# Attention and gated MLP in one kernel: in the assembling of the 64-bit weights the maximum with a constant is taken by GpSimd, beside a minimum with a very large number

## Chip, core and metric

The kernel runs on one core of one Trainium2 chip. The metric is the device time of one execution in microseconds (us). Engines are named as in the profile: PE is TensorE (matmuls), PEld its weight loads, DVE is VectorE, ACT is ScalarE, POOL is GpSimd, SP is SyncE, which here issues the DMAs.

## What is computed

The reference is a block-causal attention over 8 batches and 8 heads of 576 positions of 64 dimensions, and then a gated MLP without a nonlinearity of its own.

```python
scores = scale * np.matmul(q, k.transpose(0, 1, 3, 2))
scores = np.where(block_i >= block_j, scores, -1000000000.0)   # blocks of 64
attn = np.exp(scores - np.max(scores, axis=-1, keepdims=True))
attn = attn / (np.sum(attn, axis=-1, keepdims=True) + 1e-09)
x = np.matmul(attn, v)        # transposed and reshaped to (4608, 512)
a = x @ w1                    # 512 x 1024
b = x @ w2                    # 512 x 1024
h = a * b @ w3                # 1024 x 1024
out = (h @ w_out).astype(np.float32)   # 1024 x 512
```

The four weight matrices come in 64-bit floating point. The kernel reads them as pairs of 32-bit words and makes 32-bit values of them on the chip.

## The kernel before

The work is cut into 32 pairs of heads (`pair(n)`, four pairs to a batch). The first four pairs run beside the loading of the weights: this is the **loading stage**, some 165 us long. The generator `gen_w` goes through 40 pieces of weights of 128 x 512 values (8 of w_out, 16 of w3, 8 of w1, 8 of w2). Each piece goes through `load_w`:

- L133, a DMA issued by SP, brings 512 KB into a tile `wraw`, of which there are five;
- L138, ACT takes the absolute value of the high words into a tile `wbits`, of which there are six;
- L139, the maximum of that with 2^-15, in place;
- L140, DVE shifts the bits left by 3 and masks them;
- L141, DVE brings in the top bits of the high word;
- L144, DVE brings in the top bits of the low word; the result goes into `wo` (w_out), `w` (the w3 tile, printed as w3 in lists of instructions) or stays in `wbits`.

L139 and L140 read and write one 128 x 512 tile in SBUF; L141 and L144 read two tiles in SBUF. For w1 and w2 (`load_split`) ACT then rounds the piece (L150) and POOL subtracts the rounded from the full value (L151). For w3, PE multiplies it with w_out (L364), ACT and DVE split the product into a high and a low part (L352, L353). Beside this the first four pairs go through their attention: row maxima on DVE (L186), score and value matmuls on PE (L235, L275), exponentials on ACT (L243), splitting of q and k on ACT and POOL (L160, L209, L212), transposes on DVE (L315, L328), normalization (L329: POOL in pairs 0 and 1, DVE in pairs 2 and 3), and splitting of x (L338 on ACT, L339 on POOL).

In the loading stage the order on every engine is set by the scheduler of the language, which models the program; each engine then runs its own list in order, and an instruction that waits holds up all behind it on its engine. After the loading stage comes the **steady stage**: pairs 4 to 31 with the MLP filled in between their steps, with the order of PE written out by hand (`PLAN`).

Of the kernel before, what the change touches and what calls it, by code (L numbers as in the profile page):

```python
# [12 lines left out]
ALU = mybir.AluOpType  # L13
# [45 lines left out]
def block_causal_attention__then__gated_mlp_kernel(ctx, tc, qkv, consts, ident_in, w1, w2, w3t, wout, out_t):  # L59
    nc = tc.nc  # L60
# [64 lines left out]
    def load_w(dst, src, k):  # L125

        t = tl["early"].tile([P, 1024], F32, tag="wraw", name="wraw", bufs=5)  # L130
        u = tl["early"].tile([P, 512], F32, tag="wbits", name="wbits", bufs=6)
        wide = t.bitcast(I32)
        nc.sync.dma_start(out=wide.rearrange("p (k w) -> p k w", k=k), in_=src)  # L133
        wide = wide.rearrange("p (c two) -> p c two", two=2)
        low, high = wide[:, :, 0], wide[:, :, 1]
        bits = u.bitcast(I32)
        V = nc.vector
        nc.scalar.activation(u, high.bitcast(F32), AF.Abs)  # L138
        V.tensor_scalar(out=u, in0=u, scalar1=2.0**-15, scalar2=None, op0=ALU.max)  # L139
        V.tensor_scalar(out=bits, in0=bits, scalar1=3, scalar2=0x3FFFFFF8, op0=ALU.logical_shift_left, op1=ALU.bitwise_and)  # L140
        V.scalar_tensor_tensor(out=bits, in0=high, scalar=-0x40000000, in1=bits, op0=ALU.bitwise_and, op1=ALU.bitwise_or)  # L141
        if dst is None:
            dst = u.unsqueeze(1)
        V.scalar_tensor_tensor(out=dst.bitcast(I32), in0=low.rearrange("p (k w) -> p k w", k=k), scalar=29,  # L144
                               in1=bits.rearrange("p (k w) -> p k w", k=k), op0=ALU.logical_shift_right, op1=ALU.bitwise_or)
        return u

    def load_split(dst_h, dst_l, src):
        val = load_w(None, src.unsqueeze(1), 1)
        nc.scalar.copy(dst_h, val)  # L150
        nc.gpsimd.tensor_tensor(out=dst_l, in0=val, in1=dst_h, op=ALU.subtract)  # L151
# [190 lines left out]
    def gen_w(wp):  # L342
        wo = tl["wo"]
        for k in range(NF):
            load_w(wo[:, k : k + 1, :], wout[k * P : (k + 1) * P, :].unsqueeze(1), 1)
            yield
# [8 lines left out]
        for m in range(NF):  # L355
            t3 = wp.tile([P, NF, P], F32, tag="w3", name="w3", bufs=2)
            for k in range(0, NF, 4):
                src = w3t[k * P : (k + 4) * P, 2 * m * P : 2 * (m + 1) * P].rearrange("(k p) f -> p k f", p=P)
                load_w(t3[:, k : k + 4, :], src, 4)
                if k == 0:  # L360
                    yield
            acc = ps_m.tile([P, 512], F32, tag="psm", name=f"w{m}")
            for k in range(NF):
                nc.tensor.matmul(acc, t3[:, k, :], wo[:, k, :], start=(k == 0), stop=(k == NF - 1))  # L364
            pending.append((m, acc))
            if len(pending) > 1:
                evacuate()
            yield
            next(rows1)
            yield  # L370
# [172 lines left out]
```

## Time and profile before

| | us |
|---|---|
| median of 3 runs | 1035.99 |
| lowest and highest run | 1034.48, 1037.31 |
| the profiled execution's own time | 1035.29 |
| its span, first to last instruction | 1033.5 |

Busy time over the span: PE 977.6 us (95%), DVE 777.6 us (75%), POOL 605.2 us (59%), ACT 594.3 us (58%). A share over the whole span is an average of two stages: in the steady stage PE is busy nearly throughout, in the loading stage it is not. The table is read with the views by stretch, below.

### The profile page before, as it was taken

Reading aid. Unit: us, or ns where it says so; the run is one execution under the profiler, and the core shown is the slowest. Engines: PE = TensorE matmul, PEld = TensorE weight load, DVE = VectorE, ACT = ScalarE, POOL = GpSimd, SP = SyncE. Lnnn points to the kernel's source line nnn. Section 1 sums busy time; section 2 is a strip of 40 time slices with the busy share of each in tenths; the row PEclk is TensorE's granted clock in tenths of the full one; section 3 lists DMA queues with packets and bytes.
Section 4 is the critical chain, followed back from the end, with each engine's and each line's share of the span. In section 5 each row is a group of like instructions: output and inputs, shape, how many; then the busy total and the mean of one; then the engine's idle time right before and its main releaser. Section 6 shows DMA issues by size and latency. Waiting matters only on the chain.

```text
span 1033.5 us, 18295 instructions
## 1 busy us (share of the span) xinstructions
PE 977.6 (95%) x6624; PEld 891.3 (86%) x6624; DVE 777.6 (75%) x1376; ACT 594.3 (58%) x1505; POOL 605.2 (59%) x631
## 2 busy tenths in 40 slices
PE   2789788999999999999999999999999999999998
PEld 1444347999999999999999999999999999999998
DVE  7999997878788777778777788877777877785100
ACT  4746467666665666566565656665565566654221
POOL 3334367757676766767575767666676757673211
PEclk9889899999999999999999999999999999999999
DMA  6655421111110111111111110111111111000000
GB/s 209 220 184 182 156 94 37 37 59 37 60 36 19 43 42 55 42 54 38 60 37 60 37 50 17 42 49 43 54 38 59 36 61 36 25 1 24 1 24 23
DMA packets 27195, 61.52 MB, mean 60 GB/s; under 512 B 3360, under 2 KB 19872, under 8 KB 27104
## 3 DMA queue, kind: packets, MB, share of 16 engines
q1 hardware_dynamic: 27104, 60.35, 17.5%
q8 instruction: 52, 0.85, 0.3%
q14 instruction: 39, 0.32, 0.1%
HBM read 50.76 MB, written 9.44 MB: 58 GB/s over the span
## 4 chain that ended last, share of the span: by engine, by line
PE 53%; DVE 25%; ACT 12%; issue 7%; DMA 2%; POOL 1%; DVEq 0%; ACTq 0%; SPq 0%; POOLq 0%
PE ab L387 20%; PE o L403 17%; DVE pl L253 6%; PE s L235 6%; PE x L291 5%; DVE g L394 3%; ACT ph L251 3%; PE mx L182 3%; ACT xlow L322 2%; ACT p L250 2%; DVE wbits L141 2%; DVE m L186 2%; DVE wbits L139 2%; DVE hi L160 2%; PE w L364 1%
## 5 line engine op out<-in xcount | busy, mean ns | idle before, releaser
L256 POOL TENSOR_TENSOR rsum<-rsum,p 128x448 f32<-128x448 f32 x224 | 176.7, 789 | 117.5 <-ACT p L250 110.0
L253 DVE TENSOR_TENSOR pl<-p,ph 128x448 fp32r<-128x448 f32 x168 | 149.3, 902 | 62.6 <-ACT ph L251 61.7
L396 POOL TENSOR_TENSOR gl<-g,gh 128x288 fp32r<-128x288 f32 x128 | 111.8, 873 | 120.3 <-ACT gh L395 118.9
L395 ACT CAST gh<-g 128x288 fp32r<-128x288 f32 x128 | 55.5, 433 | 205.6 <-DVE g L394 205.6
L403 PE MATMUL o<-gh,wh 128*128 128x288 f32 x512 | 152.2, 297 | 0.0
L387 PE MATMUL ab<-xh,w1h 128*128 128x288 f32 x512 | 150.9, 295 | 1.1 <-ACT xh L338 1.1
L387 PE MATMUL ab<-xh,w2h 128*128 128x288 f32 x512 | 151.9, 297 | 0.0
L387 PE MATMUL ab<-xl,w1h 128*128 128x288 f32 x512 | 151.0, 295 | 0.5 <-POOL xl L339 0.5
L387 PE MATMUL ab<-xl,w2h 128*128 128x288 f32 x512 | 150.9, 295 | 0.0
L403 PE MATMUL o<-gh,wl 128*128 128x288 f32 x512 | 150.9, 295 | 0.0
L387 PE MATMUL ab<-xh,w1l 128*128 128x288 f32 x512 | 150.9, 295 | 0.0
L387 PE MATMUL ab<-xh,w2l 128*128 128x288 f32 x512 | 150.8, 295 | 0.0
L403 PE MATMUL o<-gl,wh 128*128 128x288 f32 x512 | 150.7, 294 | 0.0
L235 PE MATMUL s<-hi 128*128 128x288 f32 (+4 forms) x384 | 127.4, 343 | 10.9 <-ACT pe L243 7.3
L186 DVE TENSOR_REDUCE m<-mx 128x1 f32<-128x512 f32 (+6 forms) x320 | 128.6, 449 | 6.2 <-PE mx L182 2.6
L251 ACT ACTIVATE ph<-s 128x288 fp32r<-128x288 f32 x336 | 131.3, 392 | 0.0
L209 POOL TENSOR_TENSOR hi<-raw,hi 64x576 fp32r<-64x576 f32 x64 | 93.3, 1457 | 42.5 <-ACT hi L160 17.4
L291 PE MATMUL x<-ph,vs 128*128 128x256 f32 x336 | 111.3, 340 | 0.0
L250 ACT ACTIVATE p<-s 128x448 f32<-128x448 f32 x224 | 85.5, 382 | 44.9 <-PE s L235 44.6
L235 PE MATMUL s<-lo 128*128 128x288 f32 (+4 forms) x384 | 107.1, 307 | 2.2 <-DMA lo<-ms 1.2
L394 DVE TENSOR_TENSOR g<-ab,a 128x288 f32<-128x288 f32 x128 | 57.7, 451 | 67.5 <-PE ab L387 65.8
L253 DVE TENSOR_TENSOR pl<-rsum,ph 128x288 fp32r<-128x288 f32 x112 | 65.1, 582 | 48.4 <-ACT ph L251 44.6
(76 smaller groups left out, 2522.5 us busy)
## 6 DMA issues: line engine op xcount, KB each, us to landing
raw<-in_qkv SPq DMA_DIRECT2D x32, 896.0 KB
out_t<-o SPq DMA_DIRECT2D x64, 144.0 KB
wraw<-in_w3t SPq DMA_DIRECT2D x16, 512.0 KB
wraw<-in_w SPq DMA_DIRECT2D x16, 512.0 KB
wraw<-in_wout SPq DMA_DIRECT2D x8, 512.0 KB
lo<-ms SPq DMA_DIRECT2D x64, 2.2 KB
cst<-in_consts SPq DMA_DIRECT2D x1, 288.0 KB
ident<-in_ident SPq DMA_DIRECT2D x1, 128.0 KB
```

Source lines behind the costliest of these rows:

```text
L186: nc.vector.reduce_max(m[:, col : col + 1], sc, axis=AX.X)
L209: nc.gpsimd.tensor_tensor(out=hi[j][x, 1, :], in0=rqk[o, 1, :], in1=hi[j][o, 1, :], op=ALU.subtract)
L235: nc.tensor.matmul(t[ks, at : at + q1 - q0], src[:, 1, kr], src[:, 0, q0:q1], start=(s == 0), stop=(s == 1))
L250: nc.scalar.activation(p32, t[ks, at : at + w], AF.Exp, scale=SCALE)
L251: nc.scalar.activation(ph[ks, o : o + w], t[ks, at : at + w], AF.Exp, scale=SCALE)
L253: nc.vector.tensor_tensor(out=low, in0=p32, in1=ph[ks, o : o + w], op=ALU.subtract)
L256: nc.gpsimd.tensor_tensor(out=r, in0=r, in1=p32, op=ALU.add)
L291: nc.tensor.matmul(xps[:, to : to + w], v[:, c, :], pr[:, a : a + w], start=(u < 2 and s == 0), stop=(u in (0, len(PV) - 1) and s == len(p ...
L387: nc.tensor.matmul(t[:, 0:HALF], l[:, c, fs], r, start=(c == 0 and s == 0), stop=(c == NC - 1 and s == 2))
L394: nc.vector.tensor_tensor(out=g32, in0=acc[1][:, 0:HALF], in1=a32, op=ALU.mult)
L396: nc.gpsimd.tensor_tensor(out=gl[:, f, :], in0=g32, in1=gh[:, f, :], op=ALU.subtract)
L403: nc.tensor.matmul(t[:, 0:HALF], l[:, f, es], r[:, f, :], start=(f == 0 and s == 0), stop=(f == NF - 1 and s == 2))
```

## The change

One line of `load_w` is rewritten. The maximum with 2^-15 (L139) is issued on POOL instead of DVE, and the instruction takes two operations: first a minimum with 3.0e38, then the maximum. The values that come out are the same.

```diff
         V = nc.vector
         nc.scalar.activation(u, high.bitcast(F32), AF.Abs)
-        V.tensor_scalar(out=u, in0=u, scalar1=2.0**-15, scalar2=None, op0=ALU.max)
+        nc.gpsimd.tensor_scalar(out=u, in0=u, scalar1=3.0e38, scalar2=2.0**-15, op0=ALU.min, op1=ALU.max)
         V.tensor_scalar(out=bits, in0=bits, scalar1=3, scalar2=0x3FFFFFF8, op0=ALU.logical_shift_left, op1=ALU.bitwise_and)
```

The scheduler answers with another order. On DVE, at the end of pair 0's attention and the first piece of w1 (`wbits_400`), before:

```order
L328 STREAM_TRANSPOSE rb0_368<-rr0_154 128x576
L140 TENSOR_SCALAR wbits_400<-wbits_400 128x512
L139 TENSOR_SCALAR wbits_415<-wbits_415 128x512
L141 SCALAR_TENSOR_TENSOR wbits_400<-wraw_399,wbits_400 128x512
L140 TENSOR_SCALAR wbits_415<-wbits_415 128x512
L144 SCALAR_TENSOR_TENSOR wbits_400<-wraw_399,wbits_400 128x512
L141 SCALAR_TENSOR_TENSOR wbits_415<-wraw_414,wbits_415 128x512
```

And with the change, a little further on (pieces 415 to 442):

```order
L141 SCALAR_TENSOR_TENSOR wbits_415<-wraw_414,wbits_415 128x512
L144 SCALAR_TENSOR_TENSOR w3_413<-wraw_414,wbits_415 128x512
L140 TENSOR_SCALAR wbits_423<-wbits_423 128x512
L141 SCALAR_TENSOR_TENSOR wbits_423<-wraw_422,wbits_423 128x512
L353 TENSOR_TENSOR wl_83<-w0_345,wh_82 128x512
L144 SCALAR_TENSOR_TENSOR w3_413<-wraw_422,wbits_423 128x512
L140 TENSOR_SCALAR wbits_442<-wbits_442 128x512
L141 SCALAR_TENSOR_TENSOR wbits_442<-wraw_441,wbits_442 128x512
```

Before, instructions of two pieces alternate; with the change, those of one piece stand more often right behind each other. Over the loading stage 6 of these instructions stand right behind the one of the same piece whose result they read before, and 27 with the change.

On POOL, at the same place in the program (pair 0's normalization L329 and the splitting of its x, L339), with the change; before, L139 stood nowhere on POOL and the other rows followed each other in the same order:

```order
L139 TENSOR_SCALAR wbits_400<-wbits_400 128x512
L329 TENSOR_TENSOR x32_0_153<-x32_0_153,rb0_368 128x576
L139 TENSOR_SCALAR wbits_415<-wbits_415 128x512
L339 TENSOR_TENSOR xl0_0_372<-x32_0_153,xh0_0_371 128x288
L339 TENSOR_TENSOR xl0_1_376<-x32_0_153,xh0_1_375 128x288
L151 TENSOR_TENSOR w1l_81<-wbits_400,w1h_80 128x512
L139 TENSOR_SCALAR wbits_423<-wbits_423 128x512
L139 TENSOR_SCALAR wbits_442<-wbits_442 128x512
```

The maxima now stand in POOL's list behind instructions that wait for DVE (L329) and for ACT (L339, L151). In the steady stage the lists of all engines are the same as before.

## Rows read from the trace of the kernel before

**Rows 1.** The page's parts on the span and its 40 equal slices.

```profile
span 1033.5 us, 18295 instructions
...
DVE  7999997878788777778777788877777877785100
```

**Rows 2.** Busy time of each engine by stretch.

```profile
20.00:160.00 140.00, 113.12 (x344) 60.96 (x345) 132.67 (x224) 84.54 (x163) 55.51 (x37) 0.88 0.51 164
...
180.00:200.00 20.00, 19.83 (x150) 19.20 (x149) 15.60 (x32) 14.56 (x39) 13.97 (x16) 1.00 0.14 47
```

**Rows 3.** Waits from 0 to 165 us: waiter, releaser, us, times, longest.

```profile
POOL w1l L151 <- ACT w1h L150: 33.4, 6, 9.4
...
ACT wbits L138 <- DMA wraw<-in_w: 5.2, 4, 2.9
```

**Rows 4.** DVE from 0 to 180 us, groups by form: busy us, mean ns.

```profile
L141 DVE SCALAR_TENSOR_TENSOR wbits<-wraw,wbits 128x512 int32<-128x512 int32 x40 | 34.7, 872 | 0.1
L139 DVE TENSOR_SCALAR wbits<-wbits 128x512 f32<-128x512 f32 x40 | 24.7, 623 | 2.1 <-ACT wbits L138 2.0
L140 DVE TENSOR_SCALAR wbits<-wbits 128x512 int32<-128x512 int32 x40 | 19.9, 505 | 0.2
L144 DVE SCALAR_TENSOR_TENSOR w<-wraw,wbits 128x512 int32<-128x512 int32 x16 | 16.7, 1046 | 0.0
...
L144 DVE SCALAR_TENSOR_TENSOR wbits<-wraw,wbits 128x512 int32<-128x512 int32 x16 | 13.9, 868 | 0.0
```

**Rows 5.** Single lines on DVE: shortest/median/longest ns.

```profile
L139 DVE TENSOR_SCALAR wbits<-wbits x40: 407/418/1641, 15.4 to 150.1; 128x512 f32<-128x512 f32 x40
...
L140 DVE TENSOR_SCALAR wbits<-wbits x40: 369/418/1620, 18.3 to 151.7; 128x512 int32<-128x512 int32 x40
...
L141 DVE SCALAR_TENSOR_TENSOR wbits<-wraw,wbits x40: 651/681/1898, 19.1 to 152.6; 128x512 int32<-128x512 int32 x40
```

**Rows 6.** Timeline from 23 to 34 us: start us, us, engine, line, operation.

```profile
23.18 0.42 DVE L139 TENSOR_SCALAR wbits<-wbits 128x512 f32<-128x512 f32 x1
...
23.52 0.68 DVE L141 SCALAR_TENSOR_TENSOR wbits<-wraw,wbits 128x512 int32<-128x512 int32 x1
...
29.34 0.42 DVE L139 TENSOR_SCALAR wbits<-wbits 128x512 f32<-128x512 f32 x1
...
29.79 0.43 DVE L140 TENSOR_SCALAR wbits<-wbits 128x512 int32<-128x512 int32 x1
...
30.06 1.41 POOL L209 TENSOR_TENSOR hi<-raw,hi 64x576 fp32r<-64x576 f32 x1 [16.36 <-PE mx L182]
...
30.25 1.77 DVE L141 SCALAR_TENSOR_TENSOR wbits<-wraw,wbits 128x512 int32<-128x512 int32 x1
...
31.55 1.75 POOL L212 TENSOR_TENSOR lo<-raw,hi 64x576 fp32r<-64x576 f32 x1
...
31.95 1.64 DVE L139 TENSOR_SCALAR wbits<-wbits 128x512 f32<-128x512 f32 x1
```

**Rows 7.** POOL's lines in both stages: shortest/median/longest ns, first and last start.

```profile
L209 POOL TENSOR_TENSOR hi<-raw,hi x52: 1418/1422/1437, 204.7 to 919.2; 64x576 fp32r<-64x576 f32 x52
...
L396 POOL TENSOR_TENSOR gl<-g,gh x116: 792/808/1196, 202.8 to 999.6; 128x288 fp32r<-128x288 f32 x116
...
L151 POOL TENSOR_TENSOR w1l<-wbits,w1h x8: 1271/1388/2350, 54.0 to 118.5; 128x512 fp32r<-128x512 f32 x8
```

**Rows 8.** POOL groups from 0 to 180 us: the cheapest writes.

```profile
L121 POOL MEMSET pl<- 128x192 f32 x1 | 0.3, 261 | 0.0
...
L121 POOL MEMSET pl<- 128x64 f32 x1 | 0.2, 155 | 0.0
```

**Rows 9.** Timeline from 47 to 51 us, around pair 0's normalization on POOL.

```profile
47.91 0.77 DVE L328 STREAM_TRANSPOSE rb<-rr 128x576 f32<-128x576 f32 x1
...
48.85 1.40 POOL L329 TENSOR_TENSOR x<-x,rb 128x576 f32<-128x576 f32 x1 [2.67 <-DVE rb L328]
...
48.91 1.63 DVE L139 TENSOR_SCALAR wbits<-wbits 128x512 f32<-128x512 f32 x1
```

## The prediction

> **What bounds the kernel now.** I read the slices and the table by stretch first. The reader is to see two stages: DVE's digits are 9 in the slices from 26 to 155 us and 7 or 8 later [rows 1], and from 180 to 200 us PE is busy 19.83 of 20 us, while from 20 to 160 us it is busy 113.12 of 140 us and DVE 132.67 [rows 2]. So the loading stage hangs on DVE, the steady stage on PE. The changed line runs from 15.4 to 150.1 us [rows 5], inside the loading stage alone, and in the steady stage the lists of instructions are the same. The change can therefore only move the end of the loading stage, and what it moves there is handed on one for one.
>
> Next, what DVE does with its 132.67 us. The groups of the four steps of the assembling are its costliest, and their means lie far above the medians of single instructions: L139 623 ns against 418, L140 505 against 418, L141 872 against 681 [rows 4, 5]. The timeline shows where the difference comes from. POOL's L209 runs from 30.06 to 31.47 us; DVE's L141, begun at 30.25, takes 1.77 us and ends 0.55 us after L209 does. POOL's L212 starts at 31.55 and ends at 33.30; DVE's L139, begun at 31.95, ends at 33.59 [rows 6]. An instruction of this kind on DVE and an instruction on POOL that reads SBUF do not run at the same time: one waits until the other is through. I call the thing they share the port. The bill over the stage: (623 - 418) x 40 = 8.2 us for L139, (505 - 418) x 40 = 3.5 for L140, (872 - 681) x 40 = 7.6 for L141, and for L144, with L141's median, (1046 - 681) x 16 + (868 - 681) x 16 = 8.8: together 28 us of DVE's busy time are waiting for POOL.
>
> POOL was busy 55.51 us in the same stretch [rows 2], so a microsecond of POOL costs DVE 28 / 55.51 = 0.50 us. POOL's busy time contains waits of its own (L212 took 1.75 us there, its like L209 1.42 us undisturbed [rows 6, 7]); counted at durations without waits POOL's share is some 47 us (14 of the form of L209 and L212 at 1.42, 15 of L151 at 1.27, 6 at 0.81 like L396, 2 of L329 at 1.40, which are the 37 of [rows 2]; durations in [rows 7, 9]), and the price 0.60. I use 0.55.
>
> **What the change removes.** Forty L139 leave DVE. Undisturbed, the next instruction starts 0.34 us behind one (23.18 to 23.52 [rows 6]), so 40 x 0.34 = 13.6 us. Their 8.2 us of waiting for the port are not saved: the POOL instruction that blocked an L139 blocks the next L140, L141 or L144 instead.
>
> **What it adds on POOL.** No row of before shows this operation on POOL. Below: a memset, which only writes, takes 155 ns for 64 columns and 261 for 192 [rows 8], 0.83 ns a column, 527 ns for 512. Above: the two-input L151 of the same size, 1.27 us [rows 7]. Between them, by the row it is nearest to: two-input instructions take 1422 ns for 576 columns and 808 for 288 [rows 7], that is 2.13 ns a column and 194 ns fixed; with one input instead of two I take half the slope, 194 + 512 x 1.07 = 740 ns. Forty are 29.6 us of POOL, and at 0.55 they cost DVE 16.3 us; between the bounds (0.53 us at 0.50, 1.27 at 0.60) it is 10.6 to 30.5 us. POOL itself stays below its limit: 55.5 + 29.6 = 85 of 140 us.
>
> The Trainium skill (GPSIMD Engine Reference, Engine selection) says that one-input operations run on GpSimd at roughly line rate; for 512 columns at the 1.2 GHz that the page states that is an estimate of 0.43 us, with which this term would be 9.4 us and the whole sum +2 us. The same page (Elementwise side by side) gives 769 ns measured for 512 elements in a tight loop, which would leave the sum as I have it; no row here decides between them. The skill's page Perfetto Trace Analysis (Optimizing Scalar/DVE Operations) warns that moving work between GpSimd and DVE might not help because they share an SBUF read port; by that, the trace agrees, with 28 us of waiting.
>
> **What it adds on DVE.** Before, two pieces alternate on DVE and nearly no instruction waits for the one right ahead of it. Where one does, the start comes later: L139 at 29.34, its L140 at 29.79 [rows 6], 0.45 instead of 0.34 us. Such neighbours are 6 before and 27 with the change: 21 x 0.11 = 2.3 us.
>
> **What it adds by waiting in line.** POOL's list has instructions that wait long: L151 stood 33.4 us for ACT [rows 3]. That cost nothing as nobody was behind them; now the maxima are, behind each of them DVE's L140, L141 and L144 of that piece, and behind L144 the next DMA into the five wraw tiles. The first place is pair 0's normalization. From the end of rb (48.68) POOL's L329 ends at 50.25 [rows 9], then the maximum of piece 415 takes 0.74, so DVE's L140 of it can start 2.3 us after rb, and DVE has only one L144 (0.6) until then: 1.7 us idle where it now loses 1.63 - 0.42 = 1.2 us [rows 5, 9]. Then POOL has two L339 (0.81 each, by L396), L151 (1.27) and the maximum of 423 (0.74), 3.6 us, while DVE has three instructions of piece 415; with the port taken in turns DVE loses the 3.6 us, of which the price of 0.55 has charged 2.0. Together 0.5 + 1.6 = 2 us, and the same once more in pair 1: 4 us. At the other 14 L151 it is between nothing, as mostly several maxima are done ahead and row maxima stand behind, and the uncharged 0.45 x 1.27 = 0.6 us each, 8 us. I take nothing there.
>
> The DMA is not late: ACT waited 5.2 us for w1 and w2 pieces in the whole stage [rows 3]. ACT does what it did.
>
> **Sum.** -13.6 + 16.3 + 2.3 + 4.0 = +9.0 us. The profiled execution took 1035.29 us (span 1033.5 and 1.8 around it), so 1044.3; the median of the runs, 1035.99, lies 0.7 above it, so I say 1045.
>
> **Rivals.**
>
> *No change* (within 3.1 us, 0.3%, about what a measurement can tell): the POOL instruction is as quick as the memset and the waits in line are filled by other work: -13.6 + 40 x 0.53 x 0.55 + 2.3 = +0.4, 1036. For it: the memset's rate; against it: 40 instructions in line behind waits of up to 9.4 us [rows 3]. By the line rate of the Trainium skill's GPSIMD page it is this case.
>
> *Faster*: the maxima fall into times in which DVE does not need the port: its row maxima and transposes read PSUM, and it has 140 - 132.67 = 7.3 us idle. The price then is nearer 0.25 than 0.55: -13.6 + 40 x 0.53 x 0.25 + 2.3 = -6, 1030. It decides where price times duration is below (13.6 - 2.3) / 40 = 0.28 us. Against it: most instructions of DVE in the stage are the four steps, and the price of 0.50 is measured over a mix with those row maxima in it.
>
> *Much slower*: the POOL instruction costs as much as L151 or the waits in line all bite: -13.6 + 30.5 + 2.3 + 4 + 8 = +31, 1067; POOL would then be busy 106 of 140 us. For it: every arithmetic row on POOL is of this price.
>
> **Chances.** Forecast (3 to 16 us slower) 0.50, much slower 0.15, no change 0.18, faster 0.17. Slower by over 0.3% thus 0.65, within 0.18, faster 0.17. The range for 8 in 10 reaches from the faster rival's middle, 1031, to 1060, short of the worst sum; the forecast's own range is 1039 to 1052.
>
> **What would show it.** In the changed kernel's profile: L139 on POOL with a shortest duration near 0.74 us (step wrong below 0.53 or above 1.27); means of L140, L141 and L144 at least as far above their medians as now; new idle time of DVE ahead of L140 with POOL L139 as releaser, some 4 us, mostly behind L329 and L339; PE's first full stretch and the first L387 some 9 us later; the steady stage as long as now. The prediction is wrong if the excess of L140, L141 and L144 does not grow, as then the port was free when POOL wanted it, or if PE, and not DVE, ends the stage: PE's 113 us in 140 leave that room.

## The result and the profile after

Nineteen runs of the changed kernel have a median of 1037.99 us (1036.76 to 1039.90), nineteen of the kernel before beside them 1035.18 us (1034.20 to 1037.61). The ratio is 1.0023, with a 95% interval of 1.0016 to 1.0030: 2.4 us slower (here and below, differences in time are worked out from the ratios; the two medians lie 2.8 us apart). That is clear of zero, but inside the bound of 0.3% that the prediction set, so it counts as no change where +9 us was forecast. The profiled execution took 1037.76 us, its span is 1036.0 us; before it was 1033.5 [rows 1].

The two stretches of [rows 2] in the changed kernel are these (us, PE, PEld, DVE, ACT, POOL, each with its instructions, granted clock, share of DMA, GB/s).

```profile
20.00:160.00 140.00, 110.87 (x335) 58.32 (x336) 123.57 (x180) 80.71 (x156) 83.53 (x75) 0.88 0.50 162
180.00:200.00 20.00, 19.84 (x150) 19.15 (x149) 16.29 (x33) 13.68 (x35) 14.92 (x16) 1.00 0.12 40
```

DVE is relieved by 9.1 us in the loading stage and POOL loaded by 28.0 us, and yet PE does a little less in the same stretch (110.87 against 113.12). The steady stage is as full as it was. The first lines of the gated MLP's matmuls, from 160 to 300 us, before and then after (shortest, median and longest ns, first and last start in us), show that the delay at the end of the loading stage is handed on whole, 2.3 us at the first and 2.6 at the last of these 80.

```profile
L387 PE MATMUL ab<-xh,w1h x80: 288/295/398, 165.9 to 296.8; 128*128 128x288 f32 x80
```

```profile
L387 PE MATMUL ab<-xh,w1h x80: 288/295/398, 168.2 to 299.4; 128*128 128x288 f32 x80
```

The question is therefore what DVE does with the 13.6 us that it was given. Its groups by form from 0 to 180 us answer to [rows 4]: busy us, mean ns, and idle time ahead of the group with its releaser.

```profile
L141 DVE SCALAR_TENSOR_TENSOR wbits<-wraw,wbits 128x512 int32<-128x512 int32 x40 | 37.6, 951 | 0.5
L140 DVE TENSOR_SCALAR wbits<-wbits 128x512 int32<-128x512 int32 x40 | 29.0, 734 | 11.5 <-POOL wbits L139 11.5
L144 DVE SCALAR_TENSOR_TENSOR w<-wraw,wbits 128x512 int32<-128x512 int32 x16 | 15.5, 976 | 0.3
L144 DVE SCALAR_TENSOR_TENSOR wbits<-wraw,wbits 128x512 int32<-128x512 int32 x16 | 12.9, 815 | 0.2
```

Against the undisturbed 418 and 681 ns the waiting for the port inside DVE's four steps is now 12.6 us in L140, 10.8 in L141 and 7.4 in L144 (4.7, 2.1 and, for the eight of w_out with a mean of 745 ns, 0.5): 30.8 us where it was 28.2 with the same eight counted. To that comes a new thing, 11.5 us of idle time ahead of L140. The moved instruction itself, its source line and the waits around it:

```profile
L139 POOL TENSOR_SCALAR wbits<-wbits x40: 602/780/1208, 12.2 to 153.0; 128x512 f32<-128x512 f32 x40
```

```profile
DVE wbits L140 <- POOL wbits L139: 11.5, 13, 2.2
...
POOL wbits L139 <- ACT wbits L138: 22.6, 12, 5.4
```

It takes 602 ns at its shortest. DVE stands for it 13 times, at most 2.2 us. Added up: -13.6 us of DVE work, +2.6 us more waiting for the port, +11.5 us of waiting for the maxima is +0.5 us, and 21 more dependent neighbours at the prediction's 0.11 us make it +2.8, where the first L387 is 2.3 us later. The sum is not exact: it leaves out DVE's other waits, those for ACT, PE and the first DMA, which are together 2.3 us shorter than before. Counted whole up to the first L387, DVE's busy time went from 150.3 to 142.7 us and its idle time from 15.6 to 25.6 us.

### The profile page after: what moved, and what is told of

It reads as the page before. It is cut to its first block, busy times and chain, and to the rows that moved or that the text cites. A ratio compares the mean times of both kernels' runs of the same rounds, so it can differ in the third digit from the quotient of the medians.

```text
span 1036.0 us, 18299 instructions
## 1 busy us (share of the span) xinstructions
PE 976.6 (94%) x6624; PEld 889.8 (86%) x6624; DVE 769.9 (74%) x1336; ACT 592.6 (57%) x1505; POOL 634.6 (61%) x671
## 4 chain that ended last, share of the span: by engine, by line
PE 47%; DVE 26%; ACT 13%; issue 8%; POOL 3%; DMA 0%; DVEq 0%; POOLq 0%; ACTq 0%
PE ab L387 17%; PE o L403 17%; DVE pl L253 7%; PE s L235 5%; PE x L291 5%; DVE g L394 4%; ACT ph L251 3%; ACT xlow L322 2%; PE mx L182 2%; DVE wbits L141 2%; ACT p L250 2%; DVE m L186 2%; ACT gh L395 1%; DVE hi L160 1%; DVE x L329 1%
## 5 line engine op out<-in xcount | busy, mean ns | idle before, releaser
L387 PE MATMUL ab<-xh,w1h 128*128 128x288 f32 x512 | 150.9, 295 | 1.4 <-ACT xh L338 1.4
L387 PE MATMUL ab<-xh,w2h 128*128 128x288 f32 x512 | 151.8, 297 | 0.0
L387 PE MATMUL ab<-xl,w1h 128*128 128x288 f32 x512 | 151.0, 295 | 0.5 <-POOL xl L339 0.5
L387 PE MATMUL ab<-xl,w2h 128*128 128x288 f32 x512 | 150.9, 295 | 0.0
L387 PE MATMUL ab<-xh,w1l 128*128 128x288 f32 x512 | 150.9, 295 | 0.0
L387 PE MATMUL ab<-xh,w2l 128*128 128x288 f32 x512 | 150.9, 295 | 0.0
L186 DVE TENSOR_REDUCE m<-mx 128x1 f32<-128x512 f32 (+7 forms) x320 | 128.9, 449 | 6.2 <-PE mx L182 2.6
L235 PE MATMUL s<-hi 128*128 128x288 f32 (+4 forms) x384 | 125.3, 338 | 8.0 <-ACT pe L243 4.5
```

Source lines behind the costliest of these rows:

```text
L186: nc.vector.reduce_max(m[:, col : col + 1], sc, axis=AX.X)
L235: nc.tensor.matmul(t[ks, at : at + q1 - q0], src[:, 1, kr], src[:, 0, q0:q1], start=(s == 0), stop=(s == 1))
L387: nc.tensor.matmul(t[:, 0:HALF], l[:, c, fs], r, start=(c == 0 and s == 0), stop=(c == NC - 1 and s == 2))
```

## The experiments

Ten kernels ran. All but `pool_forms` were timed in turns with the kernel before on the same chip. Ratios are to it, its medians beside them were 1035.94, 1035.66 and 1035.55 us in the three groups. All edits are at L139, except for the two at L329. The theories that the texts on record weigh are the prediction's sum, its rivals, and those that they state themselves.

One thing belongs to the reading of all of them: an edit at L139 or L329 can change the scheduler's order of every list. The traces show the order of DVE's instructions up to the first L387, 213 to 215 of them with L139 left out. It is the same in the kernel before and before_spare, and in the changed kernel and single_op; one instruction stands elsewhere between no_max and no_max_spare. These three comparisons are made at one order. In the others many stand elsewhere: 53 between the kernel before and no_max, 50 between no_max_spare and the changed kernel, 61 between the kernel before and the changed one, 42 between the kernel before and before_norm_dve, 8 between the changed kernel and after_norm_dve, and 28 to 39 between the kernel before and the three kernels with a part of the maxima. What another order alone is worth, no run shows.

### What the removal, the port and the dependency are worth

**no_max** leaves the maximum out on every engine.

```diff
-        V.tensor_scalar(out=u, in0=u, scalar1=2.0**-15, scalar2=None, op0=ALU.max)
```

> The maximum is left out on every engine (it changes no value for these weights; 40 instructions leave DVE, none come to POOL). Theory A (the port: removing 40 DVE instructions is worth their 13.6 us, and the change lost that again to POOL's use of the port): 13.6 saved, 15 more dependent neighbours on DVE at 0.11 us cost 1.7, so about 12 us faster than before, 1023 to 1025. Theory B (DVE is not what the stage waits for at the margin: when it has less to do, other waits come up, PE's and ACT's): at most 4 us faster.

1022.91 us, 0.9872 (0.9853 to 0.9892): 13.2 us faster, as theory A has it; theory B's 4 us is out. **no_max_spare** leaves it out too, but lets POOL do 40 instructions of the changed kernel's form, from the high words into a region on which nobody on DVE waits (the second line of the edit is broken here).

```diff
-        V.tensor_scalar(out=u, in0=u, scalar1=2.0**-15, scalar2=None, op0=ALU.max)
+        nc.gpsimd.tensor_scalar(out=w2l[:, NC - 1, 512:], in0=high.bitcast(F32),
+            scalar1=3.0e38, scalar2=2.0**-15, op0=ALU.min, op1=ALU.max)
```

> The maximum is left out of the values, and POOL does an instruction of the same kind and size on the high words of the same piece into a part of w2l that is written over later; nothing on DVE waits for it, so this is the change without its dependency. Theory A (port price 0.55 us of DVE per us of POOL, 40 x 0.60 us): 13 us slower than the run without any maximum, about the time of the changed kernel. Theory B (POOL's work falls into gaps, the price is that DVE waits for POOL's maxima in line): within 4 us of the run without any maximum, clearly faster than the changed kernel.

1036.21 us, 1.0001 (0.9991 to 1.0012), again as theory A has it. So 40 instructions on POOL on whose result nobody on DVE waits give the whole gain back: 13.3 us. DVE's groups in no_max and then in no_max_spare, from 0 to 180 us:

```profile
L141 DVE SCALAR_TENSOR_TENSOR wbits<-wraw,wbits 128x512 int32<-128x512 int32 x40 | 35.5, 893 | 0.5
L140 DVE TENSOR_SCALAR wbits<-wbits 128x512 int32<-128x512 int32 x40 | 24.1, 608 | 4.0 <-ACT wbits L138 3.9
```

```profile
L141 DVE SCALAR_TENSOR_TENSOR wbits<-wraw,wbits 128x512 int32<-128x512 int32 x40 | 41.3, 1038 | 0.5
L140 DVE TENSOR_SCALAR wbits<-wbits 128x512 int32<-128x512 int32 x40 | 28.7, 724 | 2.1 <-ACT wbits L138 2.0
```

The spare instruction's source line (shortest, median and longest ns):

```profile
L139 POOL TENSOR_SCALAR w2l<-wraw x40: 629/856/1200, 10.2 to 141.3; 128x512 fp32r<-128x512 f32 x40
```

With the L144 rows in the same way, DVE's waiting inside its steps rises from 24.7 to 38.0 us, by 13.3, the same as the time. The price is 13.3 us for 40 x 0.629 = 25.2 us of POOL, 0.53 (0.44 to 0.62 with the intervals of both runs).

**before_spare** adds the same spare instruction to the kernel before, whose L139 stays on DVE (in the kernel both stand on the one line).

```diff
         V.tensor_scalar(out=u, in0=u, scalar1=2.0**-15, scalar2=None, op0=ALU.max)
+        nc.gpsimd.tensor_scalar(out=w2l[:, NC - 1, 512:], in0=high.bitcast(F32),
+            scalar1=3.0e38, scalar2=2.0**-15, op0=ALU.min, op1=ALU.max)
```

> The kernel before, with the maximum on DVE, and beside it on POOL 40 spare instructions of the changed kernel's kind that nobody on DVE waits for (values as before). DVE's order is the same. Theory A: 40 x 0.60 x 0.55 = 13 us slower than before; DVE's means of L139 to L144 rise by as much. Theory B: under 5 us slower.

1045.55 us, 1.0088 (1.0072 to 1.0104): +9.1 us, between the 13 of theory A and the 5 of theory B. DVE's waiting inside its steps goes from 28.2 to 37.8 us, again about as much as the time (9.6). The price of 26.0 us of POOL (40 x 0.650) is 0.35 here.

The ladder is then: removal -13.2, the port +13.3, and from no_max_spare to the changed kernel, whose DVE has to wait for the maxima, 1.0001 to 1.0023 or +2.3 us (with both intervals 0.9 to 3.6). Together +2.4. The rung of the port is measured at one order of DVE; the first and the last contain what another order is worth.

### What the form of the instruction is worth

**single_op** is the changed kernel without the minimum beside the maximum.

```diff
-        nc.gpsimd.tensor_scalar(out=u, in0=u, scalar1=3.0e38, scalar2=2.0**-15, op0=ALU.min, op1=ALU.max)
+        nc.gpsimd.tensor_scalar(out=u, in0=u, scalar1=2.0**-15, scalar2=None, op0=ALU.max)
```

> The changed kernel with the maximum alone on POOL, without the minimum beside it (same values; DVE's order is the same as in the changed kernel). If the second operation costs nothing on POOL, the shortest L139 stays at 602 ns and the time within 2 us of the changed kernel; if POOL pays for each operation, L139 gets shorter and the time falls by up to 2 us; if the form with one operation is a slower one on POOL, the time rises by 0.55 us per us of POOL (theory A).

1051.38 us, 1.0146 (1.0128 to 1.0164): +15.1 us, and 12.7 more than the changed kernel. L139's source line, and DVE's wait for it:

```profile
L139 POOL TENSOR_SCALAR wbits<-wbits x40: 1478/1538/2074, 11.9 to 163.9; 128x512 f32<-128x512 f32 x40
```

```profile
DVE wbits L140 <- POOL wbits L139: 19.7, 13, 3.0
```

One operation takes 1478 ns where two take 602. That is 40 x 0.876 = 35.0 us more of POOL for 12.7 us, a price of 0.36 where the expectation had 0.55. The minimum that looks idle is worth 12.7 us.

**pool_forms** (run once) leaves the maximum out and lets POOL write one of eight forms for each piece in turn, five of each. The edit is abridged here: the kinds 0 to 5 are given by their operations.

```diff
+        G, sp, hf = nc.gpsimd, w2l[:, NC - 1, 512:], high.bitcast(F32)
+        kind 0: max    1: min, max    2: max, min    3: mult    4: mult, add    5: add
+        kind 6: G.tensor_copy(sp, hf)    7: G.tensor_tensor(out=sp, in0=hf, in1=hf, op=ALU.subtract)
```

> The maximum is left out, as in the run without any, and POOL does a spare instruction for each piece that nobody on DVE waits for, in eight forms in turn, five of each, all reading the 128x512 high words: maximum alone, minimum and maximum, maximum and minimum, multiply alone, multiply and add, add alone, a copy, and a two-input subtraction. Theory C (a tensor_scalar with one operation takes a slow path on POOL, whatever the operation): the three forms with one operation take about 1.5 us at the shortest, the three with two operations 0.6 us. Theory D (it is the maximum as first operation that is slow): maximum alone and maximum and minimum 1.5 us, multiply alone and add alone 0.6 us. The two-input subtraction near 1.3 us in both.

1040.71 us in its one run. Its source lines 144 to 158, of that kernel alone, are the kinds 0 to 7 in their order (shortest, median and longest ns):

```profile
L144 POOL TENSOR_SCALAR w2l<-wraw x5: 1522/1782/1917, 10.5 to 119.9; 128x512 fp32r<-128x512 f32 x5
L146 POOL TENSOR_SCALAR w2l<-wraw x5: 692/804/967, 14.3 to 122.8; 128x512 fp32r<-128x512 f32 x5
L148 POOL TENSOR_SCALAR w2l<-wraw x5: 1944/2317/2487, 18.9 to 125.3; 128x512 fp32r<-128x512 f32 x5
L150 POOL TENSOR_SCALAR w2l<-wraw x5: 1529/1925/2169, 21.5 to 127.7; 128x512 fp32r<-128x512 f32 x5
L152 POOL TENSOR_SCALAR w2l<-wraw x5: 636/832/1190, 23.6 to 132.5; 128x512 fp32r<-128x512 f32 x5
L154 POOL TENSOR_SCALAR w2l<-wraw x5: 1521/1972/2037, 25.5 to 134.4; 128x512 fp32r<-128x512 f32 x5
L156 POOL CAST w2l<-wraw x5: 636/697/1020, 27.6 to 136.1; 128x512 fp32r<-128x512 f32 x5
L158 POOL TENSOR_TENSOR w2l<-wraw x5: 1042/1227/1485, 28.5 to 145.0; 128x512 fp32r<-128x512 f32 x5
```

They are read by the shortest of the five, as the longer ones can contain waits for the port. The three with one operation take 1.52 us, whichever it is; minimum with maximum takes 0.69 us, multiply with add 0.64, a copy 0.64. Maximum first and minimum second takes 1.94 us, but even its shortest, from 36.90 to 38.84 us, has one of DVE's shifts of 0.41 us wholly inside it; a multiply alone with a shift of 0.43 us inside it took 1.93 us. So this pair is as slow as one operation, and not shown to be slower. Theory C fails on this pair, theory D on multiply and add alone; the two-input subtraction, which reads one tile twice, took 1.04 us where 1.3 was expected. So it is neither that two operations cost more than one nor that a second one always makes it quick: it goes by the pair.

### Whether the waits in line at the two normalizations cost what was predicted

**before_norm_dve** and **after_norm_dve** put the normalization of pairs 0 and 1 on DVE, in the kernel before and in the changed one, so that no maximum stands behind L329 on POOL.

```diff
-        (nc.gpsimd if n < 2 else nc.vector).tensor_tensor(out=x32, in0=x32, in1=rb, op=ALU.mult)
+        nc.vector.tensor_tensor(out=x32, in0=x32, in1=rb, op=ALU.mult)
```

> The kernel before with the normalization of pairs 0 and 1 on DVE, to compare with the changed kernel after the same edit. DVE gets 2 x 1.1 us, the port gives 1.5 us back: 0 to 1 us slower than before in both theories.

> The changed kernel with the normalization of pairs 0 and 1 (L329) on DVE as in pairs 2 and 3, so that no maximum stands behind it on POOL. Waits in line, as predicted (2 us at each of the two places): 4 us less, and 2 x 1.1 us more of DVE, of which 2 x 1.4 x 0.55 = 1.5 us comes back from the port: some 3 us faster than the changed kernel. If those two places cost nothing beyond the port: within 1 us of the changed kernel, and no better against it than the kernel before with the same edit against the kernel before.

Before, it costs 0.29% (1038.75 us, 1.0029, 1.0018 to 1.0039), or 3.0 us where at most 1 was expected. In the changed kernel it costs nothing and perhaps gives a little (1037.14 us, 1.0015, 1.0004 to 1.0026, against 1.0023): 0.8 us, where 3 were expected if the waits in line cost 4.0, and less than 1 if they cost nothing. The difference of the differences, -0.37% or -3.8 us, looks like the 4.0 predicted, but most of it is the loss of before_norm_dve, where no maximum stands in line on POOL. There DVE's waits for PE up to the first L387 are 8.7 us (5.6 for L182, 3.1 for L275), 4.9 in the kernel before. And in after_norm_dve DVE's wait for the maxima did not go down with L329 off POOL's list:

```profile
DVE wbits L140 <- POOL wbits L139: 15.2, 9, 5.9
```

It is 15.2 us where it was 11.5. The agreement with the 4.0 is therefore no evidence for the waits in line; the next three runs have losses like that of before_norm_dve.

### Whether the parts add up

**wout_only**, **w3_only** and **w12_only** move the maxima of one group of pieces alone: 8, 16 and 16. In place of the line on DVE stands:

```diff
+        (nc.gpsimd.tensor_scalar(out=u, in0=u, scalar1=3.0e38, scalar2=2.0**-15, op0=ALU.min, op1=ALU.max)
+         if COND else V.tensor_scalar(out=u, in0=u, scalar1=2.0**-15, scalar2=None, op0=ALU.max))
   COND: dst is not None and k == 1 (w_out);  k == 4 (w3);  dst is None (w1, w2)
```

> Only the 8 pieces of w_out have their maximum on POOL (before pair 0's normalization, where POOL has little else to do), the other 32 on DVE. Theory A (each piece wins 0.34 us on DVE and pays 0.60 x 0.55 = 0.33 us for the port wherever it is): within 1 us of before. Theory B (the price is the place in line): these 8 have no long waits ahead of them, so 8 x 0.34 = 2.7 us faster than before.

> Only the 16 pieces of w3 have their maximum on POOL, the 24 others on DVE. Theory A (each piece wins 0.34 us on DVE and pays 0.60 x 0.55 = 0.33 us, wherever it is): within 2 us of before. Theory E (what a few pieces cost or win hangs on where POOL's instructions come to lie against DVE's and PE's, as with w_out): a ratio that does not follow the number of pieces, either side, by up to 6 us.

> Only the 16 pieces of w1 and w2 have their maximum on POOL, the 24 others on DVE. Theory A: within 2 us of before, and this run, the one with w3 and the one with w_out together add up to the changed kernel's +2.4 us. Theory E: not additive, by up to 6 us either side.

1041.84 us, 1.0056 (1.0041 to 1.0071), +5.8; 1041.22 us, 1.0052 (1.0038 to 1.0066), +5.4; 1037.21 us, 1.0013 (1.0004 to 1.0022), +1.3. The sum is +12.5, the whole is +2.4. Eight maxima cost more than forty. That is against theory A, which w12_only alone meets, and against the sum of my prediction, by which every piece costs about alike; theory B of wout_only, 2.7 us faster, is wrong too. Theory E, by which the parts do not add up, is what came, but it names no cause that could be priced. The waits of DVE up to the first L387, in the kernel before and then in wout_only, show where its time went:

```profile
DVE m L186 <- PE mx L182: 2.6, 4, 1.3
DVE tr L315 <- PE x L275: 2.3, 2, 2.1
```

```profile
DVE m L186 <- PE mx L182: 5.2, 4, 2.3
DVE tr L315 <- PE x L275: 4.8, 3, 2.4
DVE wbits L140 <- POOL wbits L139: 3.2, 3, 1.1
```

DVE's waits for PE double, from 4.9 to 10.0 us, and these 5.1 us are as much as the first L387 is later (171.0 against 165.9 us). In w3_only the same rows, with one for L364, come to 8.4 us, in w12_only to 7.7, in the changed kernel to 5.9, which is 3.5, 2.8 and 1.0 more than before; their first L387 is later by 6.9, 2.4 and 2.3 us, so that in w3_only and the changed kernel these waits are half of the delay or less. One place on the chain of waits, in the kernel before and then in wout_only: DVE's row maxima L186, the matmuls L182 that wait for them, and six matmuls of L364 ahead of the next L182; then the stretches around it in wout_only.

```profile
120.22 1.89 DVE w L144
122.11 0.61 DVE m L186
...
124.51 3.62 PE w L364 x6
```

```profile
121.04 1.89 DVE w L144
122.92 1.54 DVE wbits L140
124.46 0.33 DVE wbits L139
124.80 0.61 DVE m L186
...
127.19 4.52 PE w L364 x6
```

```profile
110.00:120.00 10.00, 2.57 (x12) 1.34 (x10) 8.74 (x16) 4.38 (x7) 2.71 (x2) 0.69 0.50 165
120.00:130.00 10.00, 7.10 (x15) 3.44 (x15) 9.54 (x15) 5.03 (x11) 4.02 (x3) 0.50 0.43 150
```

Before, the row maxima stand right behind L144. In wout_only, and in the same form in w3_only, L140 and L139 stand between them, 1.87 us, in which PE's next L182 has to wait. The six L364 then take 4.52 us, before 3.62, and the granted clock from 120 to 130 us is 0.50, the lower of its two levels (1.2 GHz), after ten microseconds in which PE was busy 2.57; before it was 0.68, after ten with 4.03 us. This reads as a chain: an order on DVE that puts the row maxima late leaves PE without work, PE then runs slower, and DVE waits for PE in turn. But the changed kernel had the clock at 0.50 in the same stretch and only 1.0 us more of such waits, so the clock alone does not tell the kernels apart. Why the parts cost more than the whole stays open. The rival that no run tests is the scheduler's order: the parts differ from the kernel before in the place of 28 to 39 of DVE's instructions, besides the maxima, and a run that holds the order fixed is missing.

## Why the prediction was wrong, point by point

*The stage and the handing on*: right. Only the loading stage moved, and the first L387 and the end moved by the same amount.

*The removal*, -13.6: right within what can be told; no_max measured -13.2 (-15.2 to -11.2), at another order of DVE. The term for dependent neighbours, 2.3, is neither confirmed nor refuted: no_max has 21 of them where the kernel before has 6, which at 0.11 us would leave 13.6 - 1.7 = 11.9, and the interval holds both.

*The price of the port*, 0.55: right in no_max_spare, 0.53. It is not a constant: 0.35 in before_spare, where DVE has its own 40 maxima besides, and 0.36 in single_op, where POOL is busy 102.9 of 140 us. Why it is lower there, no run shows.

*The duration on POOL*, 0.74 us: mis-sized, 0.602 at the shortest. It stood between the bounds, and I took half the slope of a two-input row. This term is 40 x 0.602 x 0.55 = 13.2 instead of 16.3, 3.1 us of the 6.6 by which the forecast was off (+9.0 against +2.4). The rate of the memset, 0.53 [rows 8], which I used for the rival *no change*, was nearer. The Trainium skill (GPSIMD Engine Reference, Engine selection and Elementwise side by side) was weighed there with an estimate of 0.43 us by line rate and with 769 ns measured: 0.602 lies between, so this case agrees with neither, and against a single operation, 1.478 us, both are far too low.

*Waiting in line*, 4.0: the step that failed. The ladder says so without a reading of single waits. From no_max_spare, which has 21 dependent neighbours, to the changed kernel with its 27, the prediction's terms give 6 x 0.11 = 0.7 us for neighbours and 4.0 for the waits, 4.7 in all; measured are 2.3 (0.9 to 3.6), what another order is worth included. The trace shows where the 4.0 went wrong. At pair 0's normalization the first half came as worked out: L329 ran from 50.32, the maximum behind it ended at 52.6, and DVE stood 1.88 us where 1.7 was predicted. The chain of waits of the changed kernel there runs on POOL as foreseen:

```profile
50.32 1.69 POOL x L329
52.00 0.58 POOL wbits L139
52.58 1.71 POOL xl L339 x2
54.29 1.68 POOL w1l L151
55.97 1.03 POOL wbits L139
56.99 0.02 issue
57.02 0.44 DVE wbits L140
```

What DVE lost meanwhile, changed kernel and then before, by its timeline at the same work:

```profile
52.62 1.02 DVE L140 TENSOR_SCALAR wbits<-wbits 128x512 int32<-128x512 int32 x1 [1.88 <-POOL wbits L139]
53.67 1.17 DVE L141 SCALAR_TENSOR_TENSOR wbits<-wraw,wbits 128x512 int32<-128x512 int32 x1
54.87 1.64 DVE L144 SCALAR_TENSOR_TENSOR w<-wraw,wbits 128x512 int32<-128x512 int32 x1
57.02 0.43 DVE L140 TENSOR_SCALAR wbits<-wbits 128x512 int32<-128x512 int32 x1 [0.51 <-POOL wbits L139]
```

```profile
51.05 1.02 DVE L140 TENSOR_SCALAR wbits<-wbits 128x512 int32<-128x512 int32 x1
52.00 1.28 DVE L144 SCALAR_TENSOR_TENSOR wbits<-wraw,wbits 128x512 int32<-128x512 int32 x1
...
54.14 1.75 DVE L144 SCALAR_TENSOR_TENSOR w<-wraw,wbits 128x512 int32<-128x512 int32 x1
```

The changed kernel loses 1.88 + 0.51 of idle time and 0.60 + 0.49 + 0.96 inside its steps, 4.4 us. The kernel before lost 1.2 in L139 (1.63 against 0.42 [rows 9]) and 0.60 + 0.60 + 1.07 inside these steps, 3.5 us. The place costs 0.9 us more, and the price of the port has charged 2 x 0.60 x 0.55 = 0.7 of that for its two maxima. I had added 2 us on top, taking it that all of POOL's 3.6 us behind L329 would be new, while POOL held the port there before too. At pair 1's normalization it is alike: 2.16 + 0.51 us of idle time and 1.8 inside the steps, 4.5 us, where the kernel before lost 3.5; the four maxima that POOL does there are charged 4 x 0.60 x 0.55 = 1.3. In the sum over the stage it is the same: waiting inside the steps and for the maxima is 42.3 us, and 28.2 + 13.2, the port's price alone, is 41.4. DVE that stands before L140 until POOL is through is not at the same time held up by that POOL instruction in a step of its own.

*The corrected sum*: -13.6 + 13.2 + 2.3 + 0 = +1.9 us, measured +2.4. That this comes so near is partly luck, and the 0 for the waits is one reading of the trace. By the rungs of the ladder, with the neighbours where they arise, the prediction has -13.6 + 1.7 = -11.9, +16.3 and +4.7, and the runs have -13.2, +13.3 and +2.3: the port's term was too high by 3.0 us, that of the last rung by 2.4, and the removal gave 1.3 more. What is left of the last rung beside 0.7 for neighbours, 1.6 us, can be waits or another order; no run divides it.

*The other 14 L151*, taken as nothing: no run tests them by themselves.

*Signs named beforehand*: the excess of L140, L141 and L144 grew as said for L140 and L141 and fell for L144 (8.8 to 7.4); the new idle time before L140 was to be some 4 us, mostly behind L329 and L339, and was 11.5, of which 5.1 at the two normalizations, which was the sign that waits for the port had turned into waits for the maxima. The first L387 came 2.3 us later where some 9 were said, and the steady stage stayed as long as it was. The rival *faster* needed price times duration below 0.28; it was 0.53 x 0.60 = 0.32.

*What stays open*: the sum treats the pieces alike, and the runs of the parts contradict it: by their share of the pieces in the corrected 1.9 they would cost 0.4, 0.8 and 0.8 us, and they cost 5.8, 5.4 and 1.3. Where that goes is shown for one of them (waits for PE), why they arise there and not in the whole is not. The order of the lists, which each of these edits changes, was not held fixed in any of them. The measured +2.4 of the change is that of the moved maxima together with the order that came with them.

## What to carry to other kernels

Where VectorE is the bound and shares its port with GpSimd, moving an operation from one to the other is near to a sum of zero: price the GpSimd time by the excess of VectorE's mean durations over its medians (0.50 of GpSimd's busy time by this reading; 0.53, 0.35 and 0.36 measured), and do not add the wait for GpSimd's result on top, as in the changed kernel it was largely the same time. What pays is to leave the operation out: no_max is 1.3% faster than the kernel before, at the cost of the guard for weights below 2^-127 in absolute value (the high word of 2^-127, read as a 32-bit number, is 2^-15). Where a scheduler sets the order of the lists, compare the orders before a difference of a few microseconds is put down to the edit: here the parts cost more than the whole.

## What the runs showed of the hardware that was not expected

On GpSimd a tensor_scalar of 128 x 512 with a single operation (maximum, multiply or add) took 1.48 to 1.53 us at its shortest (single_op, pool_forms), with a minimum and then a maximum 0.60 to 0.69 (changed kernel, pool_forms), with multiply and add 0.64. With a maximum and then a minimum it took 1.94 us, of which one step of DVE inside it may be 0.41. Even without that, the order of the two operations alone makes a factor over two between kinds 2 and 1 of pool_forms. That run was made once, with five instructions of each kind.
